# Boundary of two expert mixtures: a slot table read behind a weight load, and gathered rows turned later in both halves

## The chip, the cores and the metric

The kernel runs on one core of a Trainium2 chip. The time is device microseconds of one execution, taken as the median of several runs. Engines are named as in the profile: PE is TensorE (PEld its weight loads), DVE is VectorE, ACT is ScalarE, POOL is GpSimd, SP is SyncE, which here mostly issues DMAs.

## What is computed

A recurrence over 768 positions (4 sequences, 8 heads of 48) gives 3072 tokens of width 384. They go through a mixture of 8 experts with the best expert for each token, and the result through a second mixture of 8 experts with the best two for each token.

```python
def _moe_ref(x, w_gate, w_output_gate, w1, w2):
    e_idx = np.argmax(x @ w_gate, axis=1)
    ...
    for e in range(E):
        mask = e_idx == e
        h = np.maximum(x[mask] @ w1[e], 0.0)
        out[mask] = gate_w[mask, None] * eom[mask, e, None] * (h @ w2[e])

def _moe2_ref(x, w_gate, w_noise, noise, w1, w2):
    noisy_logits = x @ w_gate + np.log1p(np.exp(x @ w_noise)) * noise
    top2 = np.argpartition(-noisy_logits, 2, axis=1)[:, :2]
    ...
    for e in range(E):
        for k in range(2):
            mask = top2[:, k] == e
            out[mask] += top2_w[mask, k, None] * (np.maximum(x[mask] @ w1[e], 0.0) @ w2[e])
```

## The kernel before

The order of all work is written out by hand: each engine executes its instructions in the order in which the program emits them, and an instruction whose input or buffer is not ready holds up all that is behind it on its engine. DMAs issued by one engine are held up in the same way.

Tokens are routed to experts through tables in DRAM. For each expert a table (tab1 for mixture 1, tab2 for mixture 2) holds token numbers and weights, slot by slot. POOL writes entries with indirect DMAs (scatter, line 106), SP reads a slot range back (load1, load2, line 490), and POOL gathers the tokens' rows from `xrow` by it (gather1, gather2, line 1052). The rows are then turned: PE transposes them into a PSUM bank (line 1069), ACT copies the bank to a high part (line 1070) and DVE subtracts for the low part (line 1071). Each product of float32 values is made of three matmuls with such parts (mm3, lines 175 to 177). Weights come as four parts per expert, W1A, W1B, W2A and W2B, of 768 KB each into one of two buffers `raw` (w_load, lines 147 and 150), and are split by ACT (line 162) and DVE (line 163) in w_split. A buffer is free again when its last third has been split.

Mixture 1 runs as one loop over s (lines 1200 to 1238), with e, f = divmod(s, 8): up1(e, f) makes the hidden values of one slice f, down1 follows two slices behind, and between them lie the next expert's turning (xprep1), its weights, and the routing of the expert before: gate1 at f = 2, back1 at f = 3 and 4 (turns the output, lets ACT evacuate it, line 1152, and lets POOL scatter it to `xrow`), routing_a, routing_b, route2_c (entries for tab2) at f = 3 to 6. In the last expert, e = 7, the same slots serve the first expert of mixture 2: its W1A is loaded at f = 0, W2A at f = 1, W1B at f = 4, W2B at f = 6, and split one to three slices later (lines 1177 to 1193). load2(0, 0) at f = 0 reads the first 512 slots of expert 0 of mixture 2, gather2(xa, 0, 0) at f = 1 fetches their rows, and xprep2 at f = 5, 6, 7 turns them, one third k of the width each. It takes banks in turn from "tp", two banks that back1 also uses.

Behind the loop stand the routing of expert 7 and, between its steps, `ahead(f)`: up2(0, f, 0), the hidden values of the first 512 rows in mixture 2. Then load2(0, 1) reads the other 314 slots (line 1266), gather2(wk, 0, 1) fetches the rows (line 1331), and four down2(0, j) run on the first half (lines 1332 to 1340). Behind each of the last three stand one third of the turning of the second half (prep2(0, 3 + k)) and two steps `whole`, DVE additions over split weights (line 1297) that a later, narrow down2 needs. The loop over mixture 2's experts begins with up2(0, f, 1), which reads all three thirds. A down2 is evacuated by ACT (line 1327, three buffers `yo`) and added into the output by POOL (line 106).

Of the kernel before, what the change touches and what calls it, by code (L numbers as in the profile page):

```python
# [20 lines left out]
N, DM, E, F = B * S, H * D, 8, 1024  # L21
# [5 lines left out]
KD = DM // 128  # L27
NF = F // 128
# [36 lines left out]
def rwkv_moe_kernel(ctx, tc, r, k, v, w, rT, kT, wT, rkv, u, g1, a1, a2, g2, noise, b1, b2, out):  # L65
# [54 lines left out]
    def banks(pool, **plan):  # L120

        turns = {n: itertools.cycle(b) for n, b in plan.items()}
        return lambda name: pool.tile([128, 512], F32, name="b" + next(turns[name]))
# [46 lines left out]
    def w2_of(m, e, f, c0, c1):  # L170
        h, i = divmod(f, FH)
        return [x[:, i * DM + c0:i * DM + c1] for x in WT[m, e, 2 + h][1:]]

    def mm3(ps, st, mv, start, stop):
        nc.tensor.matmul(ps, st[0], mv[0], start=start, stop=False)  # L175
        nc.tensor.matmul(ps, st[0], mv[1], start=False, stop=False)  # L176
        nc.tensor.matmul(ps, st[1], mv[0], start=False, stop=stop)  # L177
# [304 lines left out]
    def load1(e):  # L482
        j, p = T1[e]
        j0 = 0 if e else JE
        nc.sync.dma_start(ent1[:p, e, j0:j, :], slots(0, e, j0 * p, p, j - j0))
# [7 lines left out]
    with ExitStack() as c2:  # L493
# [8 lines left out]
        bank = banks(pa, sp0="0", sp1="1", kp="2", pp="3", xp="6", lp="7")  # L502
# [537 lines left out]
    xa = ctx.enter_context(tc.tile_pool(name="xa", bufs=1))  # L1040
# [17 lines left out]
    def width(e, half):  # L1058
        return sum(T2[e][j] for j in HALF[e][half])

    def xprep2(pool, e, k, half, p):
        t = X2[e, half]
        n = width(e, half)
        if k == 0:
            for x in ("hi", "lo"):
                t[x] = pool.tile([128, KD, NH[half]], F32R, name=f"x{x}{half}")[:, :, 0:n]
        for i, j in enumerate(HALF[e][half]):
            q = T2[e][j]
            nc.tensor.transpose(p[:, i * 128:i * 128 + q], t["g"][:q, i, k * 128:(k + 1) * 128], ident[:q, :q])  # L1069
        nc.scalar.copy(t["hi"][:, k], p[:, 0:n])  # L1070
        nc.vector.tensor_tensor(t["lo"][:, k], p[:, 0:n], t["hi"][:, k].bitcast(F32), OP.subtract)  # L1071
# [10 lines left out]
    with ExitStack() as c2:  # L1082
        wk = c2.enter_context(tc.tile_pool(name="m1", bufs=2))
        bank = banks(psum, hp="01", tp="23", yp0="4", yp1="5", yp2="6", lp="7", up="01456")
# [4 lines left out]
        def part(e):  # L1089

            j, p = T1[e]
            return (range(j) if e else range(JE, j)), slice(0 if e else WE, j * p), p
# [27 lines left out]
        def up1(e, f):  # L1120
            t, c = X[e], part(e)[1]
            p = bank("hp")
            for k in range(KD):
                mm3(p[:, c], w1_of(0, e, f, k), (t["hi"][:, k, c], t["lo"][:, k, c]), k == 0, k == KD - 1)
            h = wk.tile([128, max(W1)], F32R, name="hh", bufs=4)[:, c]
            l = wk.tile([128, max(W1)], F32R, name="hl", bufs=4)[:, c]
            nc.scalar.activation(h, p[:, c], AF.Relu)
            nc.vector.scalar_tensor_tensor(l, p[:, c], 0.0, h.bitcast(F32), OP.max, OP.subtract)
            HT[e, f] = (h, l)

        def down1(e, f):
            c = part(e)[1]
            if f == 0:
                Y[e] = dict(p=[bank(f"yp{d}") for d in range(KD)])
            for d in range(KD):
                mm3(Y[e]["p"][d][:, c], w2_of(0, e, f, d * 128, (d + 1) * 128), HT[e, f], f == 0, f == NF - 1)
            if f == NF - 1:
                t = Y[e]["t"] = es.tile([128, KD, max(W1)], F32, name="yt") if e else yt0
                for d in range(KD):
                    nc.scalar.copy(t[:, d, c], Y[e]["p"][d][:, c])  # L1140
# [59 lines left out]
        for s in range(E * NF + LAG):  # L1200
            e, f = divmod(s, NF)
            if e < E:
                up1(e, f)
                if f == 6 and e + 2 < E:
                    gather1(e + 2)
                if f >= 5:
                    if e + 1 < E:
                        xprep1(e + 1, f - 5)
                    else:
                        xprep2(xa, 0, f - 5, 0, bank("tp"))  # L1210
            if s >= LAG:
                down1(*divmod(s - LAG, NF))
            if e < E:
                weights(e, f)
                if f == 0 and 0 < e < E - 2:
                    load1(e + 2)
                if f == 2 and 0 < e < 7:
                    nc.sync.dma_start(out[(e - 1) * N // 6:e * N // 6, :].rearrange("(p a) d -> p a d", p=128),
                                      z[:, None, :].to_broadcast([128, N // 6 // 128, DM]))
                if e == E - 1 and f == 0:  # L1220
                    nc.vector.tensor_copy(seen[1], base[1][:, 0:1])
                    load2(0, 0)
                if e == E - 1 and f == 1:
                    GATH += gather2(xa, 0, 0)
                if e >= 1:
                    if f == 2:
                        gate1(e - 1)
                    if f in (3, 4):
                        back1(e - 1, 2 * f - 6)
                        back1(e - 1, 2 * f - 5)  # L1230
                    if f == 3:
                        routing_a(e - 1)
                    if f == 4:
                        routing_a2(e - 1)
                    if f == 5:
                        routing_b(e - 1)
                    if f == 6:
                        route2_c(Q[e - 1], T1[e - 1][0], "tab2")
# [4 lines left out]
        e = E - 1  # L1243
# [26 lines left out]
    with ExitStack() as c2:  # L1270
        wk = c2.enter_context(tc.tile_pool(name="m2", bufs=1))
        bank = banks(psum, hp0="01", tp="23", hp1="45", yp="76")
# [3 lines left out]
        def prep2(e, i):  # L1276
            half, k = divmod(i, KD)
            xprep2(POOL[half], e, k, half, bank("tp"))
# [7 lines left out]
        def whole(e, i):  # L1286

            q = T2[e][-1]
            if quarters(q) == 1:
                return  # L1290
            if i < 6:
                h, j = divmod(i, 3)
                w, hi, lo = REST["w"][:, i * 512:(i + 1) * 512], *(x[:, j * 512:(j + 1) * 512] for x in WT[1, e, W2A + h][1:])
            else:
                c0 = (len(T2[e]) - 1) % CUT * 128
                w, hi, lo = REST["h"][:, :, 0:q], *(x[:, :, c0:c0 + q] for x in HID[1])
            nc.vector.tensor_tensor(w, hi.bitcast(F32), lo.bitcast(F32), OP.add)
# [34 lines left out]
        for j in range(CUT):  # L1332
            down2(0, j)
            if j == 0:
                for w in (W1A, W2A):
                    w_load(1, 1, w, nc.gpsimd)
            if j > 0:
                prep2(0, KD + j - 1)
                whole(0, 2 * j - 2)
                whole(0, 2 * j - 1)  # L1340
        for e in range(E):
            for f in range(NF):
                for half in range(2):
                    if e or half:
                        up2(e, f, half, bank(f"hp{half}"))
                if e and f < 3:
                    w_split(1, e, W2B, f)
                if e and f >= 2:
                    whole(e, f - 2)
                if e + 1 < E:  # L1350
                    if e and f in (0, 3):
                        w_load(1, e + 1, (W1A, W2A)[f // 3])
                    if f == 6:
                        w_load(1, e + 1, W1B)
                    if f == 0 and e + 2 < E:
                        for half in range(2):
                            load2(e + 2, half)
                    if f == 1:
                        gather2(xa, e + 1, 0)
                        gather2(wk, e + 1, 1)  # L1360
                    for part, i in SPLITS2.get(f, ()):
                        w_split(1, e + 1, part, i)
            if e == E - 2:
                left_over(wk, 1, NA)
            if e == E - 1:
                go = nc.values_load(flags[:, 2:3], min_val=0, max_val=1)
            whole(e, 6)
            js = range(0 if e else CUT, len(T2[e]))
            for n, j in enumerate(js):
                down2(e, j)  # L1370
                if e + 1 < E:
                    for i in (n,) if e else (2 * n, 2 * n + 1):
                        if i < 2 * KD:
                            prep2(e + 1, i)
                    if n < 3:
                        w_split(1, e + 1, W1B, n)
                    if n == 2:
                        w_load(1, e + 1, W2B)
# [57 lines left out]
```

## Time and profile before

| | us |
|---|---|
| median of 3 runs | 937.87 (936.85 to 938.58) |
| the profiled execution | 937.88 |
| its span on the core | 936.2 |
| PE busy | 892.2 (95% of the span) |
| DVE, ACT, POOL busy | 516.2, 395.3, 402.7 |

The profiled execution is one of the runs, so sums over its rows can be set against the median directly. Times in rows are counted from the start of the span. In the timeline a bracket behind a row gives the time that the engine sat idle before it and what released it; a row can merge several instructions (x4). PE's matmuls overlap, so the step from start to start is what one costs in a sequence. Mixture 1 ends at about 473.5 us, the branch behind it lies at 493.6, and mixture 2 fills the rest of the span.

### The profile page before, as it was taken

How to read it: one execution, taken by the hardware profiler on the slowest of the kernel's cores; microseconds unless marked ns; L12 is line 12 of the kernel's file. 1: busy time of each engine (PE TensorE's matmuls, PEld its weight loads, DVE VectorE, ACT ScalarE, POOL GpSimd, SP SyncE). 2: the span in 40 equal slices, each digit the busy share in tenths (PEclk: the TensorE clock that was granted, in tenths of full speed). 3: DMA queues.
4: the chain of work that ended last, by engine and by line, in shares of the span. 5: the costliest groups of instructions: out<-in, count | busy, mean ns of one | idle time of the engine just before them, and what ended most of it. 6: DMA issues, size and time to landing. Idle time of an engine off the chain costs nothing. (4 is left out here: it accounts for less than half of the span.)

```text
span 936.2 us, 16625 instructions
## 1 busy us (share of the span) xinstructions
PE 892.2 (95%) x6244; PEld 797.3 (85%) x6244; DVE 516.2 (55%) x1146; ACT 395.3 (42%) x862; POOL 402.7 (43%) x562
## 2 busy tenths in 40 slices
PE   8999999979799999999898999999999999999996
PEld 4887777769788999999787989889898998989995
DVE  7999999754355565556561555272543627244220
ACT  4556555333345455555441443342433425344320
POOL 3234554334244885598564441423424133242212
PEclk9999998799899999999998999999999999999998
DMA  9777664014645767676514653435444444443203
GB/s 206 180 212 181 180 172 140 28 37 132 182 124 136 183 166 174 151 185 131 160 26 106 148 134 85 76 115 104 104 88 92 133 76 122 102 102 85 34 9 44
DMA packets 91099, 113.39 MB, mean 121 GB/s; under 512 B 26002, under 2 KB 68895, under 8 KB 91000
## 3 DMA queue, kind: packets, MB, share of 16 engines
q1 hardware_dynamic: 65848, 80.87, 30.9%
q0 software_dynamic: 25152, 31.27, 18.3%
q8 instruction: 53, 0.87, 0.4%
q14 instruction: 46, 0.38, 0.2%
HBM read 86.96 MB, written 25.78 MB: 120 GB/s over the span
## 5 line engine op out<-in xcount | busy, mean ns | idle before, releaser
L106 POOL DMA_INDIRECT out<-yo,ent x54 | 84.6, 1567 | 275.6 <-ACT yo L1327 232.8
L175 PE MATMUL b<-xhi,w1h 128*128 128x512 f32 (+8 forms) x384 | 133.0, 346 | 0.0
L177 PE MATMUL b<-xhi,w1l 128*128 128x512 f32 (+8 forms) x384 | 132.1, 344 | 0.0
L176 PE MATMUL b<-xlo,w1h 128*128 128x512 f32 (+8 forms) x384 | 132.1, 344 | 0.0
L1071 DVE TENSOR_TENSOR xlo<-b,xhi 128x512 fp32r<-128x512 f32 (+8 forms) x48 | 27.1, 570 | 155.4 <-ACT xhi L1070 142.4
L1327 ACT ACTIVATE yo<-b,ent 128x384 f32<-128x384 f32 (+1 forms) x48 | 27.9, 582 | 166.8 <-issue 128.1
L1314 PE MATMUL b<-w2h,hah 128*128 128x384 f32 x256 | 88.8, 347 | 0.4 <-PEq L1262 0.4
L106 POOL DMA_INDIRECT tab<-en,si x60 | 79.8, 1330 | 19.0 <-issue 13.9
L1316 PE MATMUL b<-w2h,hal 128*128 128x384 f32 x256 | 86.9, 339 | 0.0
L1315 PE MATMUL b<-w2l,hah 128*128 128x384 f32 x256 | 86.8, 339 | 0.0
L175 PEld LDWEIGHTS b<-xhi,w1h 128*128 128x128 f32 x384 | 72.3, 188 | 11.8 <-issue 3.1
L647 POOL TENSOR_SCALAR_AFFINE_SELECT at<-at 128x512 f32<-128x512 f32 x48 | 38.8, 833 | 98.3 <-ACT at L646 98.3
L175 PE MATMUL b<-xh,w1h 128*128 128x224 f32 (+7 forms) x216 | 76.3, 353 | 3.8 <-PEq L931 3.1
L176 PEld LDWEIGHTS b<-xlo,w1h 128*128 128x128 f32 x384 | 72.4, 188 | 8.8 <-DVE xlo L1071 0.2
L177 PEld LDWEIGHTS b<-xhi,w1l 128*128 128x128 f32 x384 | 72.3, 188 | 8.6
L175 PE MATMUL b<-hh,w2h 128*128 128x224 f32 (+7 forms) x216 | 74.7, 346 | 0.0
L176 PE MATMUL b<-xl,w1h 128*128 128x224 f32 (+7 forms) x216 | 73.5, 340 | 0.1
L177 PE MATMUL b<-xh,w1l 128*128 128x224 f32 (+7 forms) x216 | 73.4, 340 | 0.0
L163 DVE TENSOR_TENSOR w1l<-raw,w1h 128x512 fp32r<-128x512 f32 x92 | 61.7, 685 | 21.0 <-ACT w1h L162 20.4
L1080 DVE SCALAR_TENSOR_TENSOR hal<-b,hah 128x512 fp32r<-128x512 f32 x64 | 44.2, 691 | 52.4 <-ACT hah L1079 52.2
L176 PE MATMUL b<-hl,w2h 128*128 128x224 f32 (+7 forms) x216 | 72.7, 336 | 0.0
L177 PE MATMUL b<-hh,w2l 128*128 128x224 f32 (+7 forms) x216 | 72.5, 336 | 0.0
(221 smaller groups left out, 2153.7 us busy)
## 6 DMA issues: line engine op xcount, KB each, us to landing
raw<-in_a SPq DMA_DIRECT2D x32, 768.0 KB, 9.5
raw<-in_b SPq DMA_DIRECT2D x30, 768.0 KB, 4.5
decay<-in_wT SPq DMA_DIRECT2D x24, 224.0 KB, 3.4
kT<-in_kT SPq DMA_DIRECT2D x24, 224.0 KB, 5.9
rT<-in_rT SPq DMA_DIRECT2D x24, 224.0 KB, 4.3
v<-in_rkv SPq DMA_DIRECT2D x24, 192.0 KB, 4.4
xrow<-x SPq DMA_DIRECT2D x24, 192.0 KB, 3.3
out<-z SPq DMA_DIRECT2D x6, 768.0 KB
```

The source lines that it names most:

```text
L106: st = nc.gpsimd.indirect_dma_start(out=table, out_offset=bass.IndirectOffsetOnAxis(ap=idx, axis=0), in_=src, in_offset=None, bounds_check ...
L163: eng.tensor_tensor(c, a, b.bitcast(F32), OP.subtract)
L175: nc.tensor.matmul(ps, st[0], mv[0], start=start, stop=False)
L176: nc.tensor.matmul(ps, st[0], mv[1], start=False, stop=False)
L177: nc.tensor.matmul(ps, st[1], mv[0], start=False, stop=stop)
L647: nc.gpsimd.affine_select(at[:, hh], at[:, hh], [[0, HP], [1, C]], OP.is_gt, 0.0, base=0, channel_multiplier=-1)
L1071: nc.vector.tensor_tensor(t["lo"][:, k], p[:, 0:n], t["hi"][:, k].bitcast(F32), OP.subtract)
L1080: nc.vector.scalar_tensor_tensor(l, p[:, 0:n], 0.0, h.bitcast(F32), OP.max, OP.subtract)
L1314: nc.tensor.matmul(parts[0], h[:, f, sl], wh, start=(f == 0), stop=False)
L1315: nc.tensor.matmul(parts[0], h[:, f, sl], wl, start=False, stop=False)
L1316: nc.tensor.matmul(parts[0], l[:, f, sl], wh, start=False, stop=(f == NF - 1))
L1327: nc.scalar.activation(o, y, AF.Copy, scale=wgt2[:q, e, j:j + 1])
```

## The change

Three orders are changed; no instruction is added or taken away.

1. In the last expert of mixture 1, the table read load2(0, 0), and the small DVE copy before it, go from f = 0 to f = 1. There they come behind weights(7, 1), which issues the load of W2A on SP, and directly ahead of gather2.
2. The three xprep2 steps of the first half go from s = 61, 62, 63 (between up1 and down1) to s = 63, 64, 65 (behind down1). The last two of these s have no up1.
3. The three prep2 steps of the second half, one behind each of down2(0, 1), down2(0, 2), down2(0, 3), become one behind down2(0, 2) and two behind down2(0, 3). They now follow the two `whole` steps of their j.

```diff
                 if f >= 5:
                     if e + 1 < E:
                         xprep1(e + 1, f - 5)
-                    else:
-                        xprep2(xa, 0, f - 5, 0, bank("tp"))
             if s >= LAG:
                 down1(*divmod(s - LAG, NF))
+            if s >= E * NF - 1:
+                xprep2(xa, 0, s - E * NF + 1, 0, bank("tp"))
             if e < E:
                 weights(e, f)
...
-                if e == E - 1 and f == 0:
+                if e == E - 1 and f == 1:
                     nc.vector.tensor_copy(seen[1], base[1][:, 0:1])
                     load2(0, 0)
-                if e == E - 1 and f == 1:
                     GATH += gather2(xa, 0, 0)
...
             if j > 0:
-                prep2(0, KD + j - 1)
                 whole(0, 2 * j - 2)
                 whole(0, 2 * j - 1)
+            for k in ((), (), (0,), (1, 2))[j]:
+                prep2(0, KD + k)
```

## Rows read from the trace of the kernel before

**Rows 1.** Busy time by stretch: span, busy per engine (count), granted clock, DMA share, GB/s
```profile
545.00:900.00 355.00, 355.00 (x2057) 322.95 (x2056) 158.79 (x279) 135.64 (x274) 107.58 (x124) 1.00 0.42 95
...
508.00:511.40 3.40, 3.40 (x13) 3.40 (x12) 1.66 (x3) 0.00 (x0) 1.64 (x2) 0.50 0.75 230
```

**Rows 2.** Timeline of PE, last expert of mixture 1: start, us, engine, line, instruction
```profile
454.80 0.33 PE L177 MATMUL b<-hh,w2l 128*128 128x372 f32 x1
457.61 0.55 PE L1151 MATMUL b<-ident,yt 128*128 128x128 f32 x3 [2.48 <-ACT x L1152]
...
459.52 0.38 PE L1069 MATMUL b<-ident,xg 128*128 128x128 f32 x2
...
461.63 0.41 PE L175 MATMUL b<-hh,w2h 128*128 128x372 f32 x1
...
465.02 0.60 PE L1069 MATMUL b<-ident,xg 128*128 128x128 f32 x4
465.37 0.42 PE L175 MATMUL b<-hh,w2h 128*128 128x372 f32 x1
```

**Rows 3.** Timeline of SP, the same stretch: DMAs as they are issued
```profile
450.70 0.35 SPq L490 DMA_DIRECT2D ent<-tab  x1
451.15 0.37 SPq L150 DMA_DIRECT2D raw<-in_b  x1
451.62 0.46 SPq L147 DMA_DIRECT2D raw<-in_b  x1
```

**Rows 4.** Timeline of POOL, the same stretch
```profile
448.60 0.96 POOL L106 DMA_INDIRECT tab<-en,si  x1 [0.21 <-issue]
454.14 1.00 POOL L1052 DMA_INDIRECT xg<-xrow,ent  x1 [4.59 <-DMA ent<-tab]
```

**Rows 5.** Timeline of DVE: last split of W2B of expert 7
```profile
440.42 0.69 DVE L163 TENSOR_TENSOR w2l<-raw,w2h 128x512 fp32r<-128x512 f32 x1
```

**Rows 6.** Timeline of ACT: first split of W2A, and evacuations of back1 behind it
```profile
455.94 1.14 ACT L162 CAST w2h<-raw 128x512 fp32r<-128x512 f32 x2 [5.82 <-DMA raw<-in_b]
456.98 1.05 ACT L1152 ACTIVATE x<-b,ent 128x384 f32<-128x384 f32 x2
```

**Rows 7.** Timeline of ACT at the end of mixture 1
```profile
472.70 1.48 ACT L1140 COPY yt<-b 128x372 f32<-128x372 f32 x3 [1.94 <-PE b L177]
```

**Rows 8.** Timeline of PE, end of mixture 1 and start of mixture 2
```profile
473.61 1.44 PE L190 MATMUL b<-yt,g2s 128*32 128x372 f32 x6
...
498.31 0.33 PE L1314 MATMUL b<-w2h,hah 128*128 128x384 f32 x1
...
502.33 0.34 PE L1316 MATMUL b<-w2h,hal 128*128 128x384 f32 x1
504.39 0.75 PE L1069 MATMUL b<-ident,xg 128*128 128x128 f32 x2 [1.72 <-DMA xg<-xrow,ent]
507.07 0.35 PE L1069 MATMUL b<-ident,xg 58*128 58x58 f32 x1 [1.94 <-DMA xg<-xrow,ent]
507.35 0.69 PE L1314 MATMUL b<-w2h,hah 128*128 128x384 f32 x1
...
518.41 0.58 PE L1069 MATMUL b<-ident,xg 128*128 128x128 f32 x3
518.92 0.41 PE L175 MATMUL b<-xhi,w1h 128*128 128x314 f32 x1
```

**Rows 9.** Chain that ended last: the last gather; timeline of DVE: the first `whole`
```profile
502.70 4.32 DMA xg<-xrow,ent
...
507.97 0.48 DVE L1071 TENSOR_TENSOR xlo<-b,xhi 128x314 fp32r<-128x314 f32 x1 [13.02 <-DMA out<-yo,ent]
508.37 1.28 DVE L1297 TENSOR_TENSOR w2f<-w2h,w2l 128x512 f32<-128x512 f32 x2
```

**Rows 10.** Timelines of DVE and POOL: a two-input operation and a scatter beside it
```profile
467.81 1.32 DVE L163 TENSOR_TENSOR w1l<-raw,w1h 128x512 fp32r<-128x512 f32 x2
...
468.41 0.97 POOL L106 DMA_INDIRECT tab<-en,si  x1 [0.21 <-issue]
```

## The prediction

> **What bounds the kernel now.** I began with the page: TensorE is busy for 95% of the span, far more than any other engine, and the chain that ended last consists mostly of PE rows. So an edit is worth what it takes out of PE's idle time or out of its half-clock time, unless something later eats it. Next I asked for the busy times after the boundary [rows 1]: from 545 to 900 us PE is busy for 355.00 of 355.00 us at a granted clock of 1.00. Nothing downstream waits for a fixed moment, so an earlier arrival there should be passed on to the end in full. The boundary, 440 to 520 us, is where PE has gaps, and the timeline of PE shows two of them.
>
> The first gap lies in the last expert of mixture 1 [rows 2]. The last matmul of down1(7, 2) starts at 454.80. A matmul of this size is followed by the next after 0.17, but the next one, a transpose of back1(6, 2), starts at 457.61. Then the transposes of the first gathered rows (line 1069) start at 459.52, and the matmul behind them only at 461.63; the same four transposes for k = 1 take 465.02 to 465.37. The second gap is in mixture 2 [rows 8]: down2(0, 1) ends at about 502.50, the transposes of the second half's rows begin at 504.39 and 507.07, and the matmuls after them step by up to 0.32 (13 are counted in 508.0 to 511.4, the first and last cut, at a granted clock of 0.50, the 1.2 GHz level [rows 1]), where before the gap 24 of them, 498.31 to 502.50, step by 0.17.
>
> Why the first gap exists is read from SP, DVE, ACT and POOL in that order. SP issues the table read load2(0, 0) at 450.70 and only then, at 451.15, the load of W2A and at 451.62 that of W1B [rows 3]. The table read must wait for the scatters to tab2, the last of which POOL issues at 448.60 [rows 4]. W2A itself could have gone long before: its buffer is read last by the split of W2B of expert 7 on DVE, 440.42 to 441.11 [rows 5]. ACT meets the missing weights at 455.94, after an idle time of 5.82, and the two evacuations of back1 that stand behind the split in its queue start at 456.98 [rows 6]. PE needs their banks, hence 457.61.
>
> **The change, part by part.** *Table read behind the load.* load2(0, 0) is one DMA of 4 KB; it and the small DVE copy of base go from f = 0 to f = 1, past one step of DVE work (that copy does not wait for anything new) and on SP past the load of W2A. No other SP step lies between. In the new order W2A can be issued at about 441.2 (440.42 + 0.69 + 0.1). In the old it took from 451.15 to 455.94, 4.79 us, with a second load beside it [rows 3, 6]; so I expect it by 446 to 448. ACT wants it at 450.1 (455.94 - 5.82). The stall of ACT disappears: PE saves 457.61 - 454.80 - 0.17 = **2.64 us** [rows 2]. The table read still waits for the same scatters, so it goes out at about 450.7 and the gathers on POOL at 454.14 as now [rows 3, 4]. Queued behind the waiting read on SP is now the load of W1B alone, issued at about 451.1; with 4.79 us it lands near 456. ACT will want it at f = 5: an estimate, from 454.97 for the new start of back1, nine matmuls of 0.17 and half a microsecond for ACT's own step, is 457. Bounds: 0 if so; if it lands 2 us later, ACT waits 1 us, but the next step behind it in ACT's queue belongs to f = 6, some 3 us on (18 matmuls of 0.17), so again 0, and beyond that one for one. I take 0.
>
> *First half turned later.* Twelve transposes, three ACT copies and three DVE subtractions go from s = 61, 62, 63 to s = 63, 64, 65 and behind down1. At s = 61 they now hold PE from 459.52 to 461.63 against 0.35 when nothing is missing; the last rows have arrived before 461.63 [rows 2]. Two steps later, near 464.5 in the new time (454.97 and some 9.5 us, three times 18 matmuls of 0.17), they are there with 3 us to spare: **1.76 us** saved. The count of PE instructions is unchanged. The third group now stands between down1(7, 7) and gate1(7). There PE waits for ACT's copies of yt in any case, which start at 472.70 and run 1.48; the gate takes 1.44 us for it (473.61 [rows 8], [rows 7]). Its 0.35 on PE is hidden there. Without that cover it would cost 0.35. ACT gets one copy of about 0.6 us (one of yt takes 0.49 [rows 7]) between yt and the gate's evacuation: it ends near 474.8, before the gate does at 475.05. DVE's subtraction, 0.69 like that of [rows 5], ends near 475.5, and back1(7, 1) wants the same bank at about 475.3, three transposes behind the gate. Bounds: +0.35 gained to 0.5 lost; I take **+0.2**, nearer to the gain, since the gate's stretch has the row.
>
> *Second half turned later.* Nine transposes, three ACT copies, three DVE subtractions; no DMA. Old: from 502.50 to the start of up2(0, 0, 1) at 518.92: 16.4 us [rows 8]. New: down2(0, 2) starts at 502.50. One down2 is 498.31 to 502.50, 4.19 us, so PE reaches the transposes of k = 0 at 506.7. The last gather lands at 507.02 [rows 9], and since routing, scatters and table read hang on the end of mixture 1 as PE does, this holds relative to PE. The third transpose therefore waits about 0.15, and down2(0, 3) starts at 507.35 to 507.45, at full clock, as PE has hardly been idle. It ends at 511.6. Six transposes: 0.51 for a group after matmuls (518.41 to 518.92 [rows 8]) and 0.35 for the next, so 512.5. Now a price is due: k = 1 and 2 are turned directly before use. ACT does the evacuation of down2(0, 3), then both copies; DVE subtracts after that, 0.48 each [rows 9]. The second and third groups of three matmuls of up2 wait for the subtraction, 0.2 us each; I take 0.4, between 0 (as at k = 0) and 1.0 (the two subtractions wholly exposed). Total 512.5 + 0.4 = 512.9 against 518.9: **6.0 us**, with ends at 4.5 (gather later by 1 and the full 1.0) and 6.5.
>
> The four `whole` steps of j = 1, 2 now stand on DVE ahead of the subtraction of k = 0 instead of behind it. Their data have long been there; the first now runs at 508.37, directly behind the subtraction at 507.97, without an idle time of its own [rows 9], so their own release is at 508.37 or earlier. If at once, they run in DVE's long idle time and cost nothing. If as late as that, four times 0.64 and the first subtraction end at 511.4, two more `whole` and two subtractions at 513.6, and up2 loses 0.9 us. DVE is idle before; I take 0.
>
> On POOL and DVE, one rule speaks against this. The row first: the scatter of 468.41 takes 0.97 us although DVE runs a two-input operation from SBUF (line 163) at 467.81 for 1.32 [rows 10]; the scatter at 448.60 takes 0.96 [rows 4]. The Trainium skill, "GPSIMD Engine Reference", section 8 (Key points), says that GpSimd shares its SBUF interfaces with VectorE and contends with DVE instructions that have two SBUF inputs; `whole` is one, and now may run beside the three gathers. By that rule four times 0.64 could push the gathers back by 2.6 us and the sum of this half would be 3.4 instead of 6.0. The row shows no such push, so the sum stays.
>
> **Sum.** 2.64 + 1.76 + 0.2 + 6.0 = 10.6 us. The profiled execution took 937.88 us (span 936.2 and 1.7 around it), 0.01 above the median of the runs, so no correction: 937.9 - 10.6 = **927.3**.
>
> **Rivals.** (a) *The second wait stays in part.* The gathers of half 1 come later relative to PE, by inserted ACT and DVE work in the routing tail or by POOL being held beside `whole`. For: no slack is left in my own sum (506.7 against 507.02). Against: the gate's wait and rows 10. Price: 2 to 2.6 us of waiting and up to 1.9 us of half clock (13 steps at 0.32 instead of 0.17); gain 6.1 to 8.6, time about 930.3.
>
> (b) *The first gap moves instead of closing.* W1B, now alone behind the table read, lands late and ACT stops at f = 5, or back1 is held by something else that ended just before the weights. Price: the 2.64, and part of the 1.76; time about 930 to 931.5. For: W1B's issue barely moves while PE comes 2.6 us earlier. Against: one load instead of two at that moment, and 2 us of room behind it.
>
> (c) *It doesn't do what it says*: both waits stay or are replaced by equal ones (ACT before f = 5, and up2 waiting for late copies): 936 to 939.
>
> (d) *Slower: the table read is late.* On SP it now stands behind the wait for W2A's buffer. Should that buffer come free after 450.7, every microsecond later delays the read, the gathers, and on POOL everything behind them: back1's scatters, routing, the second table read. PE has 3 us of room at s = 63; it pays beyond that, one for one. To lose more than the 10.6 gained, the buffer must come free after 450.7 + 3 + 10.6, about 464.3; at 468 the time would be about 941.6. Against it stands the row of 440.42 [rows 5], ten microseconds on the safe side.
>
> **How the numbers follow.** Forecast 927.3, chance 0.66, own range 925.5 to 929 (ends of the second half, 4.5 to 6.5, and of the gate, -0.5 to +0.35). Rival (a) 0.15, (b) 0.12, (c) 0.04, (d) 0.03. The range has to take in part of (a) and (b): 925.2 to 931. About 0.2% (1.9 us) is what a measurement can tell from no change: faster, below 936.0, takes the forecast, (a) and (b), 0.93; within it (c), 0.04; slower (d), 0.03.
>
> **What would show it.** Right: W2A's load on SP near 441, ahead of the table read; no wait of back1 for ACT at 455; no wait of line 1069 for the gathers in mixture 1; after down2(0, 1) no gap and a step of 0.17 throughout; up2(0, 0, 1) starting some 6 us earlier relative to the branch at the end of mixture 1; no idle PE after 545. Wrong would be: W2A still issued near 450; a wait of over 1 us at the transposes behind down2(0, 2) and steps of 0.32 after it; a stall of over 1 us inside up2(0, 0, 1) for the subtraction; or the gain present at 530 and lost before 900, for which the trace of before has no sign.

## The result and the profile after

The changed kernel takes 928.15 us (median of 11 runs) against 938.16 for the kernel before: a ratio of 0.9894, 95% interval 0.987 to 0.9919, or 10.0 us less. Forecast were 927.3, and 10.6 us less. The profiled execution has a span of 924.3 us, 11.9 less than before. 1.25 of that lies ahead of the boundary, where nothing was changed (gate1(6) starts at 445.77 instead of 447.02), so the boundary is best read in stretches of its own. Three are used from here on, all of PE.

| stretch | before | after | gained | forecast |
|---|---|---|---|---|
| S1: start of gate1(6) to start of gate1(7) | 26.59 | 22.15 | 4.44 | 4.40 |
| S2: from there to the first matmul of up2 | 2.27 | 2.06 | 0.21 | 0.2 |
| S3: start of down2(0, 0) to start of up2(0, 0, 1) | 24.88 | 19.02 | 5.86 | 6.0 |

The rows at which the stretches begin and end, in the timelines of PE before and then after (the ends of the first and the last, 473.61 and 518.92 before, stand in [rows 8], and 507.14 after stands below):

```profile
447.02 0.85 PE L190 MATMUL b<-yt,g2s 128*32 128x384 f32 x6
475.88 0.48 PE L175 MATMUL b<-xhi,w1h 128*128 128x512 f32 x1
494.04 0.41 PE L1314 MATMUL b<-w2h,hah 128*128 128x384 f32 x1 [0.45 <-PEq L1262]
```
```profile
445.77 0.85 PE L190 MATMUL b<-yt,g2s 128*32 128x384 f32 x6
467.92 1.00 PE L190 MATMUL b<-yt,g2s 128*32 128x372 f32 x6
469.98 0.48 PE L175 MATMUL b<-xhi,w1h 128*128 128x512 f32 x1
488.12 0.41 PE L1313 MATMUL b<-w2h,hah 128*128 128x384 f32 x1 [0.45 <-PEq L1261]
```

From the start of up2(0, 0, 1) to the end it is 417.16 us, 417.28 before: what was gained at the boundary reached the end whole, as the full PE rows behind it had said. Four of the experiments below (e4, e6, e7, e8) ran while every kernel took longer, the one before 950.7 us, so their whole times are set against that alone.

The waits of PE from 433 us to the end of the span (engine, line, what was waited for; total, times, longest) are now two, 0.8 us together:

```profile
PE b L1313 <- PEq L1261: 0.4, 1, 0.4
PE b L1069 <- DMA xg<-xrow,ent: 0.4, 1, 0.4
```

The timeline of SP in the last expert of mixture 1, which answers to [rows 3]:

```profile
439.89 0.38 SPq L150 DMA_DIRECT2D raw<-in_b  x1
449.50 0.34 SPq L490 DMA_DIRECT2D ent<-tab  x1
449.93 0.39 SPq L147 DMA_DIRECT2D raw<-in_b  x1
455.00 0.37 SPq L150 DMA_DIRECT2D raw<-in_b  x1
```

W2A leaves 9.6 us before the table read, which goes out 3.73 us after gate1(6), as before (3.68). The last line is W2B: its buffer is the one that W2A fills, so it now goes out 9.23 us after gate1(6) instead of 15.0. That line matters below. ACT no longer waits for weights, which answers to [rows 6]:

```profile
448.77 1.13 ACT L162 CAST w2h<-raw 128x512 fp32r<-128x512 f32 x2
450.31 1.05 ACT L1152 ACTIVATE x<-b,ent 128x384 f32<-128x384 f32 x2 [0.41 <-issue]
```

PE, which answers to [rows 2] and [rows 8] (the third and fourth lines are the first turning of the second half, the fifth the two others at once):

```profile
453.72 0.49 PE L1151 MATMUL b<-ident,yt 128*128 128x128 f32 x3
463.46 0.60 PE L1069 MATMUL b<-ident,xg 128*128 128x128 f32 x4
...
500.80 0.38 PE L1069 MATMUL b<-ident,xg 128*128 128x128 f32 x2
501.55 0.27 PE L1069 MATMUL b<-ident,xg 58*128 58x58 f32 x1 [0.37 <-DMA xg<-xrow,ent]
...
506.07 1.14 PE L1069 MATMUL b<-ident,xg 128*128 128x128 f32 x6
507.14 0.41 PE L175 MATMUL b<-xhi,w1h 128*128 128x314 f32 x1
```

back1 follows its predecessor without a wait, and the transposes of the first half find their rows. In the second half PE comes 0.4 us before the last row.

### The profile page after: what moved, and what is told of

Read it like the earlier page. It is cut to its first block, busy times and chain, and to the rows that moved or that the text cites. A ratio compares the mean times of both kernels' runs of the same rounds, so it can differ in the third digit from the quotient of the medians.

```text
span 924.3 us, 16624 instructions
## 1 busy us (share of the span) xinstructions
PE 888.1 (96%) x6244; PEld 794.7 (86%) x6244; DVE 517.5 (56%) x1146; ACT 395.5 (43%) x862; POOL 403.4 (44%) x562
## 5 line engine op out<-in xcount | busy, mean ns | idle before, releaser
L106 POOL DMA_INDIRECT tab<-en,si x60 | 79.7, 1328 | 16.2 <-issue 10.8
```

The source lines that it names most:

```text
L106: st = nc.gpsimd.indirect_dma_start(out=table, out_offset=bass.IndirectOffsetOnAxis(ap=idx, axis=0), in_=src, in_offset=None, bounds_check ...
```

## The experiments

Each is a change to the kernel before or to the changed kernel. Absolute times of single profiles differ by some microseconds ahead of the boundary, so S1, S2 and S3 are compared. e10, e11 and e12 are the same kernels as e4, e6 and e8. Each S1, S2 or S3 is of a single execution.

**Each part alone.** The diffs are the three hunks of the change. For e1, the read:

```diff
-                if e == E - 1 and f == 0:
+                if e == E - 1 and f == 1:
                     nc.vector.tensor_copy(seen[1], base[1][:, 0:1])
                     load2(0, 0)
-                if e == E - 1 and f == 1:
                     GATH += gather2(xa, 0, 0)
```

> Only the table read goes behind the load of W2A; both turnings stay where they were. Three stretches are read from the trace: S1, start of gate1(6) to start of gate1(7), 26.59 us before and 22.15 with the whole change; S2, from there to the first matmul of up2 behind routing_a, 2.27 and 2.06; S3, start of down2(0, 0) to start of up2(0, 0, 1), 24.88 and 19.02. Theory (the waits overlap): the wait of back1 for ACT (2.64) goes, but PE now reaches the transposes of the first rows 2.64 us earlier and waits there for gathers that start no earlier; S1 about 25.9 (0.4 to 1.2 gained), S2 and S3 as before, time about 937. Rival (the two savings of the first gap simply add): S1 23.95, time 935.3.

Neither: S1 rose to 30.06, 3.5 us more than before (S2 2.27, S3 25.10). The whole time can't be told from that of the kernel before (ratio 1.0015, 0.9991 to 1.0039). The timeline of PE and the busy time by stretch (granted clock third from the end):

```profile
453.50 0.30 PE L1069 MATMUL b<-ident,xg 128*128 128x128 f32 x1 [0.50 <-DMA xg<-xrow,ent]
455.60 0.33 PE L1069 MATMUL b<-ident,xg 128*128 128x128 f32 x1 [1.80 <-DMA xg<-xrow,ent]
458.55 0.98 PE L1069 MATMUL b<-ident,xg 128*128 128x128 f32 x2 [2.62 <-DMA xg<-xrow,ent]
459.18 0.66 PE L175 MATMUL b<-hh,w2h 128*128 128x372 f32 x1
459.64 0.51 PE L176 MATMUL b<-hl,w2h 128*128 128x372 f32 x1
```
```profile
458.60:464.00 5.40, 5.37 (x24) 4.79 (x25) 2.50 (x10) 1.10 (x2) 0.89 (x4) 0.54 0.18 64
```

The wait of back1 is gone, and PE stands 4.9 us at the transposes instead. Two things go beyond the theory. The clock falls after this one long wait (steps of 0.31, granted clock 0.54, so mostly the 1.2 GHz level), which it did not in [rows 2]. And the last row arrives 15.5 us after gate1(6) instead of 14.5, though its gather was issued at 11.05 instead of 11.40: it took 4.5 us from issue instead of 3.1. In that stretch W2B's load, issued at 9.25 instead of 15.0 (timeline of SP), runs beside the gathers:

```profile
452.29 0.37 SPq L150 DMA_DIRECT2D raw<-in_b  x1
```

e2, the later turning of the first half alone:

```diff
                         xprep1(e + 1, f - 5)
-                    else:
-                        xprep2(xa, 0, f - 5, 0, bank("tp"))
             if s >= LAG:
                 down1(*divmod(s - LAG, NF))
+            if s >= E * NF - 1:
+                xprep2(xa, 0, s - E * NF + 1, 0, bank("tp"))
```

> Only the three turnings of the first half go behind down1, two steps later; the table read stays ahead of W2A, the second half as before. S1, S2, S3 are the stretches named for the read alone. Theory: back1 still waits 2.64 for ACT, the transposes no longer wait: S1 24.8 (1.76 gained), S2 2.06, S3 24.88, time about 936. Rival (the later turning only pays once the weights come early, because ACT, late by the missing weights, now has the copies on top of its backlog): S1 25.6 or more, S2 2.3 or more.

S1 26.91, S2 2.05, S3 25.07; ratio 0.9993 (0.9968 to 1.0018). The wait for the rows is gone as expected, the wait of back1 stays, and the 1.76 that should have been gained did not come. PE's timeline and the busy time by stretch of e2:

```profile
457.58 0.90 PE L1151 MATMUL b<-ident,yt 128*128 128x128 f32 x3 [2.29 <-ACT x L1152]
458.13 0.66 PE L175 MATMUL b<-xh,w1h 128*128 128x372 f32 x1
```
```profile
457.60:460.00 2.40, 2.40 (x9) 2.40 (x10) 1.65 (x10) 1.93 (x6) 2.14 (x4) 0.50 0.68 220
```

A granted clock of 0.50 again, and steps of 0.31, after an idle time of 2.29. In the kernel before the step from 457.61 to 459.52 covers three transposes and nine matmuls, which is full clock, after 2.48. The same gap, 2.1 to 2.7 us long, is followed by the low level in e2, e4, e5 and e10 and not in before and e3: four of six profiles. Where it is, and the transposes still stand in their old place (e5), S1 hardly changes (26.44): the slower PE only arrives later at rows that were late anyway.

The clock is not what decides S1 in e2, though. Behind these matmuls PE waits a third time, for the routing on DVE. Timelines of DVE (the last step of the routing, line 337) and of PE (the first matmul of routing_b, line 219), of the kernel before, of e2 and of the changed kernel:

```profile
462.99 0.20 DVE L337 TENSOR_TENSOR ob<-oc,valid 128x24 bf16<-128x24 f32 x1
463.25 0.23 PE L219 MATMUL b<-ob,ones 128*128 128x8 bf16 x3
```
```profile
463.00 0.21 DVE L337 TENSOR_TENSOR ob<-oc,valid 128x24 bf16<-128x24 f32 x1
463.27 0.23 PE L219 MATMUL b<-ob,ones 128*128 128x8 bf16 x3 [0.56 <-DVE ob L337]
```
```profile
455.96 0.18 DVE L337 TENSOR_TENSOR ob<-oc,valid 128x24 bf16<-128x24 f32 x1
457.11 0.23 PE L219 MATMUL b<-ob,ones 128*128 128x8 bf16 x3
```

On DVE the routing stands behind the first split of W2A. From the start of that split to line 337 it is 6.40 to 6.44 us in the kernel before, e2, e3 and e10, and PE's matmul follows 0.26 to 0.27 later in all four: 15.9 to 16.2 us after gate1(6). e3, where the clock held, waits 0.55 there. In the kernel before, the wait for the rows hid this. So with W2A late, PE gets no further however early the transposes are out of its way, at either level of the clock, and the later turning alone can gain nothing. With the change DVE is done before PE comes, at 11.3 after gate1(6). The rival as I wrote it named ACT and the copies; the engine is DVE, but that the later turning only pays once the weights come early is what the rows show. Its number for S1 came out, that for S2 did not.

e3, the second half alone:

```diff
             if j > 0:
-                prep2(0, KD + j - 1)
                 whole(0, 2 * j - 2)
                 whole(0, 2 * j - 1)
+            for k in ((), (), (0,), (1, 2))[j]:
+                prep2(0, KD + k)
```

> Only the second half's turnings go behind down2(0, 2) and down2(0, 3); mixture 1 as before. Theory: S1 26.59 and S2 2.27 as before; S3 19.0 (5.9 gained: about 4 us of waiting and 1.9 of half clock), time about 932. Rival (the gain of the second half hangs on the first, because the gathers would be late without it): S3 20.5 or more and a wait of over 1.5 us at the transposes.

S1 26.30, S2 2.28, S3 18.97, a wait of 0.33 at the transposes; 931.33 us, ratio 0.993 (0.989 to 0.9971). The theory holds: this part is independent of the others.

**The change without the read** (e4, and again e10): e2 and e3 together.

> The whole change without the table read: both turnings later, load2(0, 0) ahead of W2A as before. Theory: the wait of back1 for ACT stays; S1 24.6 (2.4 to 2.6 more than with the whole change), S2 about 2.1, S3 19.0; time about 2.5 us above the whole change. Rival (the later turning alone takes both waits, the read brings nothing): S1 22.2.

> Once more the whole change without the table read. Theory: the wait of back1 for ACT is 2.1 to 2.7 us and now nothing behind it absorbs what follows from it: S1 24.4 to 24.8 where the clock holds, 26.4 to 27 where it falls after the wait; 3 to 5 us between this and the whole change. Rival (the read is worth nothing once the turnings are late): S1 22.2.

e10: S1 26.73, S2 2.05, S3 19.0; 933.09 us, ratio 0.9932 (0.9908 to 0.9957). e4 had S1 28.11, S3 18.96 and a ratio of 0.9937 (0.9887 to 0.9987): the wait that was expected, 2.66, but with a fall of the clock that was not. In e10 the wait is 2.12, the clock falls behind it, and PE then waits 0.58 for the routing, as PE's timeline shows:

```profile
457.25 0.90 PE L1151 MATMUL b<-ident,yt 128*128 128x128 f32 x3 [2.12 <-ACT x L1152]
...
458.25 0.51 PE L176 MATMUL b<-xl,w1h 128*128 128x372 f32 x1
...
462.93 0.23 PE L219 MATMUL b<-ob,ones 128*128 128x8 bf16 x3 [0.58 <-DVE ob L337]
```

So the read alone loses 3.5 us of S1, the later turning alone gains nothing, and both together gain 4.44. With e10 as the base, the read is worth 26.73 - 22.15 = 4.6 us. All of it lies ahead of the routing matmul, which comes 15.91 us after gate1(6) in e10 and 11.34 with the change. By whole times, an estimate from the two ratios (0.9932 and 0.9894), it is 3.6 us.

**Is it waiting that lowers the clock?** e5: the kernel before with PE kept busy through the second gap.

```diff
+                if j == 1:
+                    spare = bank("hp0")
+                    for f in range(20):
+                        nc.tensor.matmul(spare[:, 0:DM], HID[0][0][:, f % NF, 0:128], w2_of(1, 0, f % NF, 0, DM)[0],
+                                         start=True, stop=True)
                 prep2(0, KD + j - 1)
```

> The kernel before, with 20 extra matmuls of 128x384 (results unused, 3.5 us at full clock) between down2(0, 1) and the transposes that wait for the gather, into a bank that is free. Theory (the matmuls behind the second gap run at 1.2 GHz because PE had nothing to do in it): the extra work lies wholly inside the wait of 4.4 us, the clock stays at 2.4 GHz, down2(0, 2) steps by 0.17 from its first matmul, and S3 falls from 24.88 to about 23.0 although PE does more; time about 936. Rival (the clock falls for another reason, such as the DMAs or the transposes): steps of 0.32 stay, S3 24.9 or more.

S3 22.97, with 20 matmuls more; 935.75 us, ratio 0.9971 (0.9947 to 0.9995). PE and the granted clock behind the gap:

```profile
502.24 0.38 PE L1069 MATMUL b<-ident,xg 128*128 128x128 f32 x2
503.43 0.27 PE L1069 MATMUL b<-ident,xg 58*128 58x58 f32 x1 [0.81 <-DMA xg<-xrow,ent]
503.62 0.44 PE L1314 MATMUL b<-w2h,hah 128*128 128x384 f32 x1
503.90 0.33 PE L1315 MATMUL b<-w2l,hah 128*128 128x384 f32 x1
```
```profile
503.40:508.00 4.60, 4.58 (x26) 4.48 (x27) 1.69 (x3) 0.42 (x1) 2.32 (x4) 1.00 0.92 247
```

Steps of 0.17 and a granted clock of 1.00, while the DMAs are as busy as before. Of the 5.9 us of the second half 1.9 were half clock and 4.0 waiting.

e9 tried the same on e1:

```diff
                     else:
+                        if f == 5:
+                            spare = bank("lp")
+                            for i in range(24):
+                                nc.tensor.matmul(spare[:, 0:372], w1_of(0, e, 0, i % KD)[0], X[e]["hi"][:, i % KD, 0:372],
+                                                 start=True, stop=True)
                         xprep2(xa, 0, f - 5, 0, bank("tp"))
```

> The read alone, with 24 extra matmuls of 128x372 (results unused, about 4.1 us at full clock) in PE's queue ahead of the first transposes of mixture 1's end, where PE waited 4.9 us for the gathered rows and then ran 12 matmuls at 1.2 GHz. Theory (the read alone lost because all of PE's waiting lies in one place and the clock falls): no steps of 0.31 behind the transposes, S1 falls from 30.06 to 27.5 to 28.5 although PE does 4.1 us more. Rival (the rows come later than in the kernel before, and that alone is the loss): S1 29.5 or more.

S1 29.92, ratio 1.0006 (0.9974 to 1.0038). The number is the rival's. The filler ran at full clock up to 459.7, but the last row came later still, 16.35 us after gate1(6) (timeline of PE):

```profile
460.36 0.33 PE L1069 MATMUL b<-ident,xg 128*128 128x128 f32 x1 [0.30 <-DMA xg<-xrow,ent]
462.12 0.33 PE L1069 MATMUL b<-ident,xg 128*128 128x128 f32 x1 [1.43 <-DMA xg<-xrow,ent]
```

Its gather had been issued at 456.17, 5.95 us before. And after an idle time of only 0.30 and 1.43 the clock fell again (0.62 from 464 to 467). So the read alone loses by late rows and by the clock, and PE's rows tell how much by each. The last row's transpose comes 14.53 us after gate1(6) in the kernel before, 15.51 in e1 and 16.35 in e9: 1.0 and 1.8 by late rows. From there to the transposes of k = 1 PE takes 3.47 before, 5.95 in e1 and 4.98 in e9: 2.5 and 1.5 by the clock. What the filler saved on the clock was lost on the rows; whether it made them later was not tested.

**The room at s = 63.** e8, and again e12: the changed kernel with the read and the gathers at f = 4, behind W1B's load on SP and back1's scatters on POOL.

```diff
-                if e == E - 1 and f == 1:
-                    nc.vector.tensor_copy(seen[1], base[1][:, 0:1])
-                    load2(0, 0)
-                    GATH += gather2(xa, 0, 0)
...
+                    if e == E - 1 and f == 4:
+                        nc.vector.tensor_copy(seen[1], base[1][:, 0:1])
+                        load2(0, 0)
+                        GATH += gather2(xa, 0, 0)
                     if f == 5:
                         routing_b(e - 1)
```

> The changed kernel, with the table read and the four gathers at f = 4 instead of f = 1: behind the load of W1B on SP and behind back1's scatters on POOL. The read goes out no later (it waits for the scatters to tab2), but the gathers start about 3.8 us later (about 3.8 us more after gate1(6) than the 6.7 of the changed kernel). Theory (PE has about 3 us of room at s = 63): PE waits 0.4 to 1.5 us at the first transposes of mixture 1's end, S1 22.6 to 23.7. Rival (the room is larger): no wait, S1 22.15.

> Once more the changed kernel with the table read and gathers at f = 4. Theory: gathers start 12.3 us after gate1(6), the last lands 19.7 after it, PE wants it at 17.7: 1.2 to 2 us of waiting, S1 23.4 to 24.4. Rival (the waits of the first look came from a disturbed chip): no wait, S1 22.15.

e12 was worse than either: S1 29.04, 6.9 us more than with the change. The gathers start 15.1 us after gate1(6) instead of 6.7, PE waits four times at the first transposes, 3.5 us together, and the clock falls (timeline of PE, then busy time by stretch, of e12):

```profile
466.99 0.33 PE L1069 MATMUL b<-ident,xg 128*128 128x128 f32 x1 [0.82 <-DMA xg<-xrow,ent]
...
470.83 0.48 PE L1069 MATMUL b<-ident,xg 128*128 128x128 f32 x1 [0.83 <-DMA xg<-xrow,ent]
473.90 1.06 PE L1069 MATMUL b<-ident,xg 128*128 128x128 f32 x4
```
```profile
471.00:474.00 3.00, 3.00 (x11) 2.92 (x12) 1.89 (x3) 1.62 (x3) 2.53 (x5) 0.50 0.05 3
```

In e8 the gathers started 12.3 us after gate1(6) and PE waited 1.2 us, as expected of it; S1 is 24.37, above the range, since the transposes took 1.7 us longer for these waits and gate1(7) came another 0.5 later. This is the mechanism of my rival (d) at work, by another cause than the buffer. In this order the gathers also stand behind back1's scatters into the same table of rows, and in e8 the landing of such a scatter is what the first gather waited for (timeline of POOL):

```profile
466.06 1.01 POOL L1052 DMA_INDIRECT xg<-xrow,ent  x1 [1.64 <-DMA xrow<-x,ent]
```

What held e12's gathers, 8.4 us later than with the change, is not settled: the profile names a split on DVE, which they do not read.

**DVE beside POOL.** e6, and again e11: the four additions `whole` behind the turning of k = 0 instead of ahead of it.

```diff
-            if j > 0:
-                whole(0, 2 * j - 2)
-                whole(0, 2 * j - 1)
+            if j == 3:
+                whole(0, 4)
+                whole(0, 5)
             for k in ((), (), (0,), (1, 2))[j]:
                 prep2(0, KD + k)
+            if j == 2:
+                for i in range(4):
+                    whole(0, i)
```

> The changed kernel, with the four additions `whole` of j = 1 and 2 behind the turning of k = 0 instead of ahead of it, so that DVE has nothing to do while POOL issues the three gathers. Theory (DVE's two-input work does not hold POOL's gathers): the gathers take 1.0 to 1.1 and 1.26 us each and start 6.2 us after down2(0, 0) as with the change (6.25), and the wait of line 1069 stays at 0.3 to 0.4 us. Rival (DVE and POOL hinder each other): the first gather falls from 1.10 to 1.00 us, the last lands earlier and the wait falls below 0.2 us. Either way S3 stays within 0.4 us of 19.02.

> Once more the changed kernel with four `whole` behind the turning of k = 0. Theory (DVE and POOL hinder each other a little): first gather 1.00 us instead of 1.10, the wait of line 1069 in the second half 0.1 to 0.3 instead of 0.37, S3 18.9 to 19.0. Rival: 1.10 and 0.37 as with the change.

With the change, DVE runs the additions beside the first gather; in e11 it runs nothing there. POOL and then DVE of the changed kernel:

```profile
494.37 1.10 POOL L1052 DMA_INDIRECT xg<-xrow,ent  x1 [5.70 <-DMA ent<-tab]
```
```profile
493.31 2.50 DVE L1296 TENSOR_TENSOR w2f<-w2h,w2l 128x512 f32<-128x512 f32 x4 [4.27 <-ACT yo L1326]
```

POOL and then PE of e11:

```profile
495.73 1.00 POOL L1052 DMA_INDIRECT xg<-xrow,ent  x1 [5.60 <-DMA ent<-tab]
```
```profile
502.24 0.70 PE L1069 MATMUL b<-ident,xg 128*128 128x128 f32 x3
```

The gather takes 1.00 instead of 1.10 and the wait of 0.37 is gone, more than expected: S3 18.68, 0.34 less than with the change (a single execution, 927.13 us; 0.3 us is less than whole times can tell). In e7, below, the second gather lies almost wholly beside six additions and takes 1.48 us instead of 0.97. Beside the same additions the first gather takes 1.15 in e3, and with DVE idle 1.00 in the kernel before. So the additions hold up a gather beside them, by 0.1 to 0.5 us. They are not slowed themselves: six take 3.70 us beside gathers (e7) and 3.69 without (e11). Not every gather is held up: one of e3 in mixture 1, at 455.39, takes 0.96 though a split starts on DVE at 455.78. In e6 the first gather took 1.00 as well, and the wait was 0.49.

**All three turnings last.** e7, the changed kernel with `((), (), (), (0, 1, 2))[j]`.

> The changed kernel, with all three turnings of the second half behind down2(0, 3). Theory: the wait of 0.37 us for the gather goes, nine transposes in a row cost the same PE time, but up2(0, 0, 1) then waits for the copies and subtractions of k = 0 too: 0.3 to 1 us, S3 18.9 to 19.8, the time the same within the measurement. Rival (the copies keep up, as they did for six transposes): S3 18.6.

S3 19.17, against 19.02; ratio 0.9934 (0.9877 to 0.9991). The wait for the gather is gone, and another takes its place, but not the one named (timeline of PE): the third group of transposes waits for a bank, since "tp" has two and the subtraction of k = 0 has not emptied the first.

```profile
516.29 1.14 PE L1069 MATMUL b<-ident,xg 128*128 128x128 f32 x6
518.01 0.64 PE L1069 MATMUL b<-ident,xg 128*128 128x128 f32 x3 [0.57 <-DVE xlo L1071]
```

## Why the prediction was right, point by point

*The bound.* PE's rows behind the boundary were full, and the gain came through whole. Right.

*Read behind the load, 2.64.* W2A goes out at 439.89, 5.88 us ahead of gate1(6); the forecast was 441.2, or 5.8 ahead. ACT's wait and back1's wait are gone. Right in the whole change. But the sum took this and the 1.76 of the turning as two terms that can each be had. They cannot: e1 alone gives -3.5, e2 alone -0.3, both 4.44. The early read alone moves PE's wait to the rows, and the late turning alone moves it to the routing on DVE, which hangs on W2A as back1 does and which the prediction did not name. The forecast of the whole did not suffer, as both edits were in it and the early W2A brings the routing forward too; as a statement on each part it was wrong.

*W1B behind the waiting read, 0.* Right: ACT splits it at 456.15 without a wait. *What I left out* is W2B: W2A's early split frees its buffer early, and W2B's load then goes out at 9.2 instead of 15.0 after gate1(6), into the gathers. "3 us to spare" at s = 63 rests on rows at the old arrival of 14.5. With the new order of loads the last rows came at 15.5 (e1), 16.4 (e9) and, in the changed kernel itself, 16.5 (the last gather, issued at 456.33, lands 5.9 us later), and PE wants them at 17.7: the room is 1.2 to 2.2 us. That it was enough is luck, as the sum had not looked there. From issue to landing, or to the transpose that waited for it, the last gather takes 3.1 to 3.5 us in before, e2, e3 and e10, where W2B's load starts after it, and 4.5 to 5.95 in e1, the changed kernel and e9, where the load starts 1.2 to 1.8 us ahead of it. That the load causes this is argued from these times; no run moved W2B alone.

*First half's tail, +0.2.* 0.21. Right, including its reason: gate1(7) takes 1.00 instead of 1.44 [rows 8], since PE turns the last third while ACT copies yt.

*Second half, 6.0.* 5.86, and 0.1 more inside up2. Three sizes in it were off and cancelled. The wait at k = 0 was 0.37, not 0.15. The six transposes took 1.07, not 0.86. The stall of up2 for the subtractions, 0.4, did not come: its first nine matmuls take 1.49 us, 1.59 before.

*The additions and the rule of the skill.* The additions started at 493.31, with the first evacuation by ACT, not at once and not as late as [rows 9] allowed. My row for "no push" [rows 10] was one scatter. The Trainium skill, "GPSIMD Engine Reference", section 8 (Key points), says that GpSimd contends with DVE instructions that have two SBUF inputs. The traces agree: a gather takes 1.10 with the change against 1.00 in e11, and 1.48 in e7 against 0.97. That the shared interfaces are the reason is not shown. Its size is far from the bound of 2.6 us that I had worked out; here it cost 0.3, by the single execution of e11.

*Rivals.* (a) occurred in its smallest form, 0.4 us of wait with no fall of the clock. (b) and (c) did not occur. (d) did not either, but e12 shows that its price per microsecond was set too low: I had PE pay one for one, and behind such a wait it pays for the half clock too.

## What to carry to other kernels

Two waits of the same engine in a row are not two terms of a sum: before adding them, work out each edit alone, since taking the first away may only lengthen the second, or worse, lead to one long stand behind which the clock falls, and taking the second away may lay bare a third that it hid. Follow everything that hangs on the late input, on every engine, and not only the wait that is seen. A load moved earlier frees its buffer earlier and pulls the next load forward with it; follow that one to what it runs beside. Work that can be put between a gather and its use can be worth more than its own wait: in the second half 1.9 of the 5.9 us were half clock (e5). In e9 it brought nothing.

## What was not expected of the hardware

The same gap of PE, 2.1 to 2.7 us long, was followed by the 1.2 GHz level in four profiles (e2, e4, e5, e10) and by full clock in two (before, e3). In e9 it fell after two waits of 0.30 and 1.43 us, in e12 during four of 0.82 to 1.00, with a transpose between each. Where it fell, the three transposes and nine matmuls behind the gap took 3.4 to 3.5 us (e2, e5, e10) instead of 1.9, and one profile does not tell whether it will. In these three S1 did not pay for it, since the rows or the routing were late anyway. The first gather of the second half takes POOL 1.00 us with DVE idle and 1.10 to 1.15 beside two-input additions; another took 1.48 instead of 0.97.
